# Convolution mixer on one core: the first group's background work is counted at 1.2 times its VectorE time by the planner

## The chip, the core and the metric

The kernel runs on one NeuronCore of a Trainium2 chip. The metric is the device time of one execution in microseconds (us). Three executions of the kernel before gave 2064.7 to 2065.62 us, with a median of 2064.75 us.

## What is computed

The input `x` is (8, 4096, 192) in float32: 8 batches, 4096 tokens, 192 channels. There are three stages.

```python
# 1. causal convolution, 7 taps, one softmaxed filter for each of 8 heads of 24 channels
w = softmax(weight)                                   # (8, 7)
c = einsum('hk,bskhg->bshg', w, windows(x, 7))        # (8, 4096, 192)
# 2. token mixing, weights 4096x256 and 256x4096
u = c + (relu(c.T @ w_tok1) @ w_tok2).T
# 3. channel mixing, weights 192x1536 and 1536x192
out = u + relu(u @ w_ch1) @ w_ch2
```

The four weight matrices arrive as 64-bit floats. The kernel reads them as pairs of 32-bit words and builds float32 values from them on VectorE and ScalarE.

## The kernel before, in words

**Groups and tiles.** The batches are worked on in five groups, `[[0], [1], [2, 3], [4, 5], [6, 7]]`. Within a group the 4096 tokens are cut into 8 tiles of 512. The text below numbers the tiles of the first group (batch 0) 0 to 7 and those of the second group (batch 1) 8 to 15. Each tile goes through the same steps on TensorE (PE):

- `channel1` (L934): 108 matmuls into pairs of PSUM buffers, six pairs. ScalarE (ACT) makes the rounded half `hh` (L973) of each result and VectorE (DVE) the remainder `hl` (L974). One pool of six PSUM buffers, `ps_x`, serves all steps of a tile.
- `mix2` (L861 and L862) for the *next* tile: four blocks of four matmuls each, with the token weights `w_tok2` as the stationary operand. In the first group they come from `t2s`, an SBUF buffer that holds a high part (written by ACT, L185) and a low part (written by DVE, L186). In later groups they come from DRAM as `t`. DVE adds the result to `u` (L876, L877).
- half of `channel2` (L1008, L1009), then `transposed` (L894, with `own` written by ACT at L896 and by DVE at L897) for the next tile, then the other half of `channel2`. DVE adds the results into `osb` (L1012, L1013).

**Background work.** While the first group runs, the kernel must also prepare the second: the convolution of batch 1 on DVE (192 taps at L633; the first tap of each head is on ACT, L631), the first token product of batch 1 on PE (L721), the decoding of the rest of `w_tok2` (12 jobs, each with four steps into `dec_top` at L172, L173, L176, L179 and a last one into the low part of `t2s`, L186), and the copies of the decoded weights to DRAM (`stage`, L1111 on ACT; `t2d`, L1113 on SyncE). In the same manner the second group prepares the third, and so on.

**The planner.** Each engine runs its instructions in the order in which the program was written, so the order is fixed when the kernel is built. A class `Background` decides where a background item goes. It keeps two running sums in nanoseconds, `pe` and `dve`, of the work written so far. After each piece of foreground work, `fg` adds its cost and `fill` puts in items until the DVE sum stands `until` ahead of the PE sum:

```python
if self.dve >= self.pe + until:
    ready = [s for s in ready if s["items"][0].pe]
```

An item of two taps has the cost `2 * (RB * nb * G / 0.96 + 130)`, 660 ns for one batch. Two calls do not ask the budget: `finish(group)` puts in all that is left of a group, and `require(tag)` puts in the items of a stream up to the one with that tag. `require` stands in the first group just ahead of `mix2`, and names the part of `t2s` that this `mix2` reads; each tile of the first group needs two decode jobs more than the tile before it:

```python
if gi == 0 and nxt[0] == 0:
    bg.require(("t2", nxt[1] // 2, nxt[1] % 2))
mix2(*nxt, *loaded)
```

Of the kernel before, what the change touches and what calls it, by code (L numbers as in the profile page):

```python
# [34 lines left out]
class Background:  # L35
# [9 lines left out]
        self.pe = 0.0  # L45
        self.dve = 0.0

    def add(self, items, lead=0.0, group=None):
        total = sum(it.cost for it in items) or 1.0
        self.streams.append(dict(items=items, total=total, done=0.0, free=self.pe, lead=lead, group=group))  # L50

# [63 lines left out]
def conv_mixer_kernel(ctx: ExitStack, tc: tile.TileContext, x, weight, w_tok1, w_tok2, w_ch1, w_ch2, out):  # L115
# [16 lines left out]
    TT = TJ * P  # L132
# [3 lines left out]

    AHEAD = {1: 5, 2: 3}
    LAST = NJ // MJ - 3
    ST = RB * P

    def f32(ap):
        return ap.bitcast(F32)
# [7 lines left out]
    bg = Background()  # L150
# [94 lines left out]
    def t2_job(q2, a0, na, kc=None):  # L245

        c0 = q2 * ST + a0
        cs = slice(2 * c0, 2 * (c0 + na))
# [22 lines left out]
    def decode_items(dec, jobs, loaded=False):  # L271


        n = dec.n / 0.96
        sts = [{} for _ in jobs]
        items = []

        def add(cost, lag, fn, tag=None, gate=None, eager=False):
            items.append(Item(fn, cost + (190 if cost else 0), lag, gate=gate, tag=tag, eager=eager))

        def load(i):
            def fn():
                jb = sts[i]["jb"] = jobs[i][0]()
                sts[i]["raw"] = jb.get("raw") or dec.load(jb["src"], jb["shape"])

            if i < len(jobs):
                add(0, 0, fn, eager=True)

        def begin(i):
            def fn():  # L290
                sts[i]["a"] = dec.a(sts[i], sts[i]["jb"].get("top", lambda: None)())

            if i < len(jobs):
                add(0, 12e3 if i == 0 and not loaded else 0, fn, eager=loaded and i == 0)

        def high(i):
            if not jobs[i][4]:
                return

            def fn():  # L300
                jb = sts[i]["jb"]
                hi, lo = jb["make"]() if "make" in jb else (jb["hi"], jb["lo"])
                sts[i]["b"] = dec.b(sts[i], hi, lo, jb.get("view", lambda v: v))

            add(0, 0, fn, gate=jobs[i][3])

        def low(i):
            def post():
                if "post" in sts[i]["jb"]:
                    sts[i]["jb"]["post"]()  # L310

            if jobs[i][4]:
                add(n, 0, lambda: sts[i]["b"][0](), jobs[i][1])
            add(0, 0, post, jobs[i][1])
            items.extend(jobs[i][2])

        load(0)
        load(1)
        begin(0)
        for i in range(len(jobs)):  # L320
            if i:
                high(i - 1)
            for k, c in enumerate((0.5, 0.5, 1, 1)):
                add(n * c, 500 if k == 0 else 0, lambda i=i, k=k: sts[i]["a"][k]())
                if k == 0 and i:
                    low(i - 1)
                if k == 2:
                    begin(i + 1)
            load(i + 2)
        high(len(jobs) - 1)  # L330
        add(0, 500, lambda: None)
        low(len(jobs) - 1)
        return items
# [264 lines left out]
    def stage1(gi, pools):  # L598
        bs = GROUPS[gi]
        nb = len(bs)  # L600
        convolving, mixing, accs = [], [], []
# [10 lines left out]
        def load(q2, part):  # L612
# [3 lines left out]
            for i, b in enumerate(bs):  # L616

                at = (b * S + q2 * ST - HALO) * D + ds.start
                assert at >= 0
# [40 lines left out]
        def t1_load(n):  # L660
            q2, q = divmod(n, RB // MJ)
            js = slice(q * MJ, (q + 1) * MJ)

            def part(d):
                return d[q2 * ST:(q2 + 1) * ST].rearrange("(p j) t m -> p j t m", j=RB)[:, js]

            top = t1d.rearrange("s (t m) -> s t m", t=1)
            if nb == 1:
                t1 = mp.tile([P, MJ, 1, JT], F32, name="t1", bufs=AHEAD[nb] + 1)
                nc.sync.dma_start(out=t1, in_=part(top))  # L670
            elif gi == 2:
                if n < LAST:
                    t1 = mp.tile([P, MJ, 2, JT], F32R, name="t1", bufs=AHEAD[nb])
                else:

                    if "spare" not in done:
                        done["spare"] = mp.tile([P, 2, ND, TT], F32R, name="other").rearrange("p a c t -> p (a c t)")
                    w = MJ * 2 * JT
                    t1 = done["spare"][:, (n - LAST) * w:(n - LAST + 1) * w].rearrange("p (j t m) -> p j t m", t=2, m=JT)
                nc.sync.dma_start(out=f32(t1[:, :, 1:2]), in_=part(top))  # L680
            else:
                t1 = mp.tile([P, MJ, 2, JT], F32R, name="t1", bufs=AHEAD[nb])
                nc.sync.dma_start(out=f32(t1), in_=part(t1p))
            states[q2]["t1", q] = t1
            mark("t1", n)
# [5 lines left out]
        def t1_lo(q2, q):  # L691
# [3 lines left out]
            nc.gpsimd.dma_start(  # L695
                out=t1p[q2 * ST:(q2 + 1) * ST].rearrange("(p j) t m -> p j t m", j=RB)[:, js], in_=f32(t1)
            )
# [61 lines left out]
        def multiply(*a):  # L759
# [7 lines left out]
            for kc in range(KC):  # L767
# [3 lines left out]
                mixing.append(it)  # L771
            if n + AHEAD[nb] < (LAST if gi == 2 else NJ // MJ):
                mixing.append(Item(lambda: t1_load(n + AHEAD[nb])))
            if gi == 2 and n % 2 and n // 2 < NJ // MJ - LAST:
                mixing.append(Item(lambda: t1_load(LAST + n // 2)))

# [25 lines left out]
            bg.finish(gi)  # L802
            mix1_done(gi, accs)

        bg.add(convolving, group=gi)
        bg.add(second, group=gi)
        return start, finish

# [5 lines left out]
    def t2s_of(q2):  # L814
        if q2 not in t2s:
            t2s[q2] = t2sp[q2 % 2].tile([P, KC, 2, ST], F32R, name="t2s")
        return t2s[q2]
# [236 lines left out]
    td = decode_ctx.enter_context(tc.tile_pool(name="td", bufs=1, side="right", reuse_waits="tile"))  # L1054
# [5 lines left out]
    def first_items():  # L1060

        jobs, stores = [], []
        state = {}

        def decoded(q2):
            state["t2", q2] = max(bg.pe, bg.dve)

        def stored(q2):
            state["stored", q2] = bg.pe

        decoded(0)
        for q2 in range(NS):
            for kc in range(KC):
                for r in range(2):
                    a = (q2, kc, r)
                    stores.append(Item(lambda a=a: store_t2(*a, 0), lag=1000, gate=lambda q2=q2: state.get(("t2", q2))))
                    stores.append(Item(lambda a=a: store_t2(*a, 1), lag=600))
                    stores.append(Item(lambda a=a: store_t2(*a, 2), lag=1200))
            stores.append(Item(lambda q2=q2: stored(q2)))
            for a0 in range(0, ST, TT) if q2 else []:  # L1080
                for kc in range(KC):
                    after = []
                    if a0 + TT == ST and kc == KC - 1:
                        after.append(Item(lambda q2=q2: decoded(q2)))

                    def gate(q2=q2):
                        if q2 > 1 and (mixed[0] <= 2 * (q2 - 2) or ("stored", q2 - 2) not in state):
                            return None
                        return 0.0

                    jobs.append((lambda a=(q2, a0, TT, kc): t2_job(*a), ("t2", q2, a0 // TT), after, gate, True))
        def through():

            decode_ctx.close()
            conv_pool(0)
            starts[2] = stage1(2, lambda k: cps[k])

        stores.append(Item(through))
        bg.add(decode_items(Decoder(td, TT, 2, 2), jobs), lead=0.1, group=1)
        bg.add(stores, group=1)  # L1100

    t2p = []
# [1 line left out]
    def store_t2(q2, kc, r, step):  # L1104

        if step == 0:
            t2p.append(td.tile([P, 2 * TT], F32R, name="stage", bufs=2).rearrange("m (j p) -> m j p", j=RB))
        if step < 2:
            js = slice(step * RB // 2, (step + 1) * RB // 2)
            v = f32(t2s[q2][:, kc, r]).rearrange("m (p j) -> m j p", j=RB)  # L1110
            nc.scalar.copy(out=t2p[-1][:, js], in_=v[:, js])  # L1111
        else:
            nc.sync.dma_start(out=t2d[q2][:, kc, r], in_=f32(t2p[-1]))  # L1113

    def conv_pool(k):
        cps[k] = ctx.enter_context(tc.tile_pool(name=f"cp{k}", bufs=1, reuse_waits="tile"))

    def run_ahead(gi):

        if gi and gi + 2 < len(GROUPS) and gi + 2 not in starts and bg.idle():  # L1120
            starts[gi + 2] = stage1(gi + 2, lambda k: cps[k])
# [101 lines left out]
```

## Time and profile before

| | |
|---|---|
| median of three runs | 2064.75 us (2064.7 to 2065.62) |
| the profiled execution's own time | 2066.69 us |
| its span, first to last instruction | 2064.8 us |
| PE busy | 2052.5 us, 99% of the span |
| DVE busy | 1404.0 us, 68% |
| ACT busy | 760.2 us, 37% |
| mean granted clock of PE | 0.999 |
| the chain that ended last | PE 90%, DVE 6%, DMA 2%, ACT 1% |

The profiled execution's span is 1.9 us shorter than its own time and equal to the median of the three runs to within 0.1 us. "Busy" of PE counts a matmul until its modelled end, and matmuls overlap, so a PE that waits a little can still read as busy. The length of a tile, from the first matmul of its `channel1` to that of the next tile, is the better measure.

### The profile page before, as it was taken

How to read it: one execution, taken by the hardware profiler on the slowest of the kernel's cores; microseconds unless marked ns; L12 is line 12 of the kernel's file. 1: busy time of each engine (PE TensorE's matmuls, PEld its weight loads, DVE VectorE, ACT ScalarE, POOL GpSimd, SP SyncE). 2: the span in 40 equal slices, each digit the busy share in tenths (PEclk: the TensorE clock that was granted, in tenths of full speed). 3: DMA queues.
4: the chain of work that ended last, by engine and by line, in shares of the span. 5: the costliest groups of instructions: out<-in, count | busy, mean ns of one | idle time of the engine just before them, and what ended most of it. 6: DMA issues, size and time to landing. Idle time of an engine off the chain costs nothing.

```text
span 2064.8 us, 41285 instructions
## 1 busy us (share of the span) xinstructions
PE 2052.5 (99%) x17723; PEld 1902.8 (92%) x17723; DVE 1404.0 (68%) x2781; ACT 760.2 (37%) x1305; POOL 101.7 (5%) x167
## 2 busy tenths in 40 slices
PE   9999999999999999999999999999999999999999
PEld 9889999998989989999999999999999999999998
DVE  8899979999559988448965778444445444444444
ACT  4656544434333333224323433233223232233222
POOL 0100000000000000000000000000000000000000
PEclk9999999999999999999999999999999999999999
DMA  9855436554354564232543433322211212222210
GB/s 308 291 154 183 138 120 197 180 164 137 132 160 136 177 170 132 78 103 74 151 124 90 129 122 108 98 60 67 67 45 52 65 50 67 59 67 67 67 32 17
DMA packets 259654, 239.44 MB, mean 116 GB/s; under 512 B 202832, under 2 KB 213584, under 8 KB 257936
## 3 DMA queue, kind: packets, MB, share of 16 engines
q1 hardware_dynamic: 243616, 158.55, 26.6%
q0 software_dynamic: 15856, 78.26, 11.8%
q8 instruction: 140, 2.29, 0.4%
q14 instruction: 42, 0.34, 0.1%
HBM read 146.60 MB, written 71.30 MB: 106 GB/s over the span
## 4 chain that ended last, share of the span: by engine, by line
PE 90%; DVE 6%; DMA 2%; ACT 1%; issue 1%; SPq 0%; POOL 0%; ACTq 0%; POOLq 0%
PE ps_x L934 35%; PE ps_x L1008 16%; PE ps_x L991 16%; PE ps_x L1009 7%; DVE xc L633 2%; PE ps_x L894 2%; PE ps_x L864 2%; PE ps_a L725 2%; PE ps_x L866 2%; PE ps_a L726 2%; PE ps_a L727 2%; PE ps_x L865 2%; DVE hl L974 1%; PE ps_a L426 1%; DMA t2d<-stage 1%; DMA dec_raw<-in_moe_w_tok_dram 1%
## 5 line engine op out<-in xcount | busy, mean ns | idle before, releaser
L973 ACT ACTIVATE hh<-ps_x 128x512 fp32r<-128x512 f32 x756 | 411.1, 597 | 807.2 <-PE ps_x L934 807.1
L974 DVE SCALAR_TENSOR_TENSOR hl<-ps_x,hh 128x512 fp32r<-128x512 f32 x756 | 485.1, 685 | 218.2 <-ACT hh L973 217.7
L934 PE MATMUL ps_x<-own,w_hi 64*128 64x512 f32 x2880 | 607.6, 390 | 1.4 <-DVE hl L974 1.2
L1008 PE MATMUL ps_x<-w,hh 128*128 128x384 f32 x1872 | 542.6, 361 | 0.7 <-DVE hl L974 0.6
L934 PEld LDWEIGHTS ps_x<-own,w_hi 64*128 64x128 f32 x2880 | 429.4, 184 | 55.9 <-issue 6.5
L1009 PE MATMUL ps_x<-w,hl 128*128 128x192 f32 x1872 | 468.8, 250 | 0.0
L934 PE MATMUL ps_x<-other,w_hi 64*128 64x512 f32 x1728 | 450.9, 389 | 0.5 <-DVE osb L1013 0.3
L633 DVE SCALAR_TENSOR_TENSOR xc<-raw,cw,xc 128x384 f32<-128x384 f32 (+1 forms) x768 | 388.7, 561 | 9.2 <-ACT xc L631 9.2
L1009 PEld LDWEIGHTS ps_x<-w,hl 128*128 128x128 f32 x1872 | 357.5, 191 | 0.0
L1008 PEld LDWEIGHTS ps_x<-w,hh 128*128 128x128 f32 x1872 | 351.4, 188 | 1.5 <-DVE hl L974 1.5
L934 PEld LDWEIGHTS ps_x<-other,w_hi 64*128 64x128 f32 x1728 | 314.0, 184 | 33.9 <-DVE hl L974 1.8
L991 PE MATMUL ps_x<-w,hh 64*128 64x384 f32 x2304 | 329.9, 355 | 0.0
L934 PE MATMUL ps_x<-own,w_lo 64*128 64x512 f32 x1440 | 326.5, 387 | 0.0
L991 PE MATMUL ps_x<-w,hl 64*128 64x192 f32 x2304 | 292.2, 247 | 0.1
L934 PE MATMUL ps_x<-other,w_lo 64*128 64x512 f32 x864 | 242.1, 386 | 0.0
L934 PEld LDWEIGHTS ps_x<-own,w_lo 64*128 64x128 f32 x1440 | 218.1, 184 | 24.4
L991 PEld LDWEIGHTS ps_x<-w,hl 64*128 64x128 f32 x2304 | 223.4, 188 | 1.7 <-DVE hl L974 0.8
L991 PEld LDWEIGHTS ps_x<-w,hh 64*128 64x128 f32 x2304 | 219.5, 184 | 0.9
L1012 DVE TENSOR_TENSOR osb<-ps_x,u 128x192 f32<-128x192 f32 x156 | 55.4, 355 | 205.1 <-PE ps_x L1009 204.9
L934 PEld LDWEIGHTS ps_x<-other,w_lo 64*128 64x128 f32 x864 | 159.0, 184 | 16.7
L896 ACT CAST own<-ps_x 128x512 fp32r<-128x512 f32 x120 | 63.4, 595 | 268.7 <-PE ps_x L894 268.5
L999 DVE TENSOR_TENSOR osb<-ps_x,osb 128x192 f32<-128x192 f32 x288 | 103.0, 358 | 17.0 <-DVE osb L999 0.5
(135 smaller groups left out, 1880.4 us busy)
## 6 DMA issues: line engine op xcount, KB each, us to landing
raw<-in_x_dram SPq DMA_DIRECT2D x56, 672.0 KB, 7.4
t<-t2d SPq DMA_DIRECT2D x64, 512.0 KB, 5.0
out_dram<-osb POOLq DMA_DIRECT2D x63, 384.0 KB, 4.3
u<-xcd SPq DMA_DIRECT2D x62, 384.0 KB, 5.6
xcd<-xc POOLq DMA_DIRECT2D x28, 768.0 KB, 7.4
other<-own POOLq DMA_DIRECT2D x24, 768.0 KB, 5.4
t<-t1p SPq DMA_DIRECT2D x32, 512.0 KB, 4.1
t2d<-stage SPq DMA_DIRECT2D x16, 512.0 KB, 4.3
```

The costliest lines, as they stand in the source:

```text
L633: nc.vector.scalar_tensor_tensor(out=dst, in0=src, scalar=cw[:, h, k:k + 1], in1=dst, op0=ALU.mult, op1=ALU.add)
L725: nc.tensor.matmul(out=ps, lhsT=wh, rhs=xh, start=a, stop=False)
L726: nc.tensor.matmul(out=ps, lhsT=wh, rhs=xl, start=False, stop=False)
L896: nc.scalar.copy(out=own[:, 0, c], in_=ps)
L934: nc.tensor.matmul(out=ps, lhsT=w1[w][rows, c, p * P:(p + 1) * P], rhs=t[h][rows, v, c], start=n == 0, stop=n == len(prods) - 1,)
L973: nc.scalar.activation(out=h["hh", f], in_=ps, func=AF.Relu)
L974: nc.vector.scalar_tensor_tensor(out=h["hl", f], in0=ps, scalar=0.0, in1=f32(h["hh", f]), op0=ALU.max, op1=ALU.subtract)
L991: nc.tensor.matmul(out=ps[:, :m], lhsT=h[part, f][ks, ts], rhs=w2[ks, f, :m], start=n == 0 and part == "hh", stop=z and part == "hl",)
L999: nc.vector.tensor_tensor(out=osb[:, j], in0=v, in1=osb[:, j], op=ALU.add)
L1008: nc.tensor.matmul(out=ps[:, :2 * D], lhsT=h["hh", f][:, ts], rhs=w2[:, f, :], start=n == 0, stop=False)
L1009: nc.tensor.matmul(out=ps[:, :D], lhsT=h["hl", f][:, ts], rhs=w2[:, f, :D], start=False, stop=z)
L1012: nc.vector.tensor_tensor(out=rows(osb[:, j]), in0=rows(ps[:, :D]), in1=tokens(u, i)[:, j], op=ALU.add)
```

## The change

`Background.add` gets a factor `pace`, by which the cost of each item of the stream is multiplied. Two streams of the second group get 1.2: the convolution of batch 1 (all but its second raw load, a stream of its own without cost) and the decoding of `w_tok2`. An item of two taps then counts 792 ns instead of 660. What the items compute does not change, and nothing is added to or taken from the program; only the place of the instructions moves.

```diff
-    def add(self, items, lead=0.0, group=None):
+    def add(self, items, lead=0.0, group=None, pace=1.0):
+
+        for it in items:
+            it.cost *= pace
         total = sum(it.cost for it in items) or 1.0
...
+    PACE = 1.2
...
-        bg.add(convolving, group=gi)
+        bg.add(convolving, group=gi, pace=PACE if gi == 1 else 1.0)
         bg.add(second, group=gi)
...
-        bg.add(decode_items(Decoder(td, TT, 2, 2), jobs), lead=0.1, group=1)
+        bg.add(decode_items(Decoder(td, TT, 2, 2), jobs), lead=0.1, group=1, pace=PACE)
```

On every engine the order is the same up to the end of tile 0 and again from the last tile of the second group on. Line numbers behind the edit are four higher in the changed kernel (L974 is L978, L633 is L637). Three places follow.

The first place is DVE at the end of tile 0 and the beginning of `channel1` of tile 1. `xc` rows are taps of the convolution, `osb` is the last sum of tile 0, and the first `hl` row is the first remainder of tile 1. Before:

```order
L633 SCALAR_TENSOR_TENSOR xc_897<-raw_765,cw,xc_897 128x8x24 x2
L957 TENSOR_TENSOR osb<-ps_x,u 128x192
L172 TENSOR_SCALAR dec_top<-dec_top 128x512
L186 TENSOR_TENSOR t2s<-dec_top,t2s 128x512
L173 TENSOR_SCALAR dec_top<-dec_top 128x512
L176 SCALAR_TENSOR_TENSOR dec_top<-dec_raw,dec_top 128x512
L633 SCALAR_TENSOR_TENSOR xc_897<-raw_765,cw,xc_897 128x8x24 x2
L957 TENSOR_TENSOR osb<-ps_x,u 128x192
L633 SCALAR_TENSOR_TENSOR xc_897<-raw_765,cw,xc_897 128x8x24 x2
L179 SCALAR_TENSOR_TENSOR dec_top<-dec_raw,dec_top 128x512
L633 SCALAR_TENSOR_TENSOR xc_897<-raw_765,cw,xc_897 128x8x24 x4
L974 SCALAR_TENSOR_TENSOR hl_934<-ps_x,hh_933 128x512 x2
```

The same stretch in the changed kernel:

```order
L961 TENSOR_TENSOR osb<-ps_x,u 128x192
L637 SCALAR_TENSOR_TENSOR xc_903<-raw_765,cw,xc_903 128x8x24 x2
L176 TENSOR_SCALAR dec_top<-dec_top 128x512
L190 TENSOR_TENSOR t2s<-dec_top,t2s 128x512
L177 TENSOR_SCALAR dec_top<-dec_top 128x512
L180 SCALAR_TENSOR_TENSOR dec_top<-dec_raw,dec_top 128x512
L961 TENSOR_TENSOR osb<-ps_x,u 128x192
L637 SCALAR_TENSOR_TENSOR xc_903<-raw_765,cw,xc_903 128x8x24 x4
L183 SCALAR_TENSOR_TENSOR dec_top<-dec_raw,dec_top 128x512
L978 SCALAR_TENSOR_TENSOR hl_931<-ps_x,hh_930 128x512 x2
```

Ten taps stood ahead of the first `hl`; now there are six.

The second place is DVE in `channel1` of tile 2. The row that writes `t2s` is the last step of the decode job that `mix2` behind this `channel1` reads, in the changed kernel; in the kernel before, that job was done earlier and this row belongs to the next tile's part. Before, from the third `hl` pair to the sixth:

```order
L974 SCALAR_TENSOR_TENSOR hl_1321<-ps_x,hh_1320 128x512 x2
L186 TENSOR_TENSOR t2s<-dec_top,t2s 128x512
L974 SCALAR_TENSOR_TENSOR hl_1323<-ps_x,hh_1322 128x512 x2
L633 SCALAR_TENSOR_TENSOR xc_897<-raw_768,cw,xc_897 128x8x24 x2
L974 SCALAR_TENSOR_TENSOR hl_1323<-ps_x,hh_1322 128x512 x2
L633 SCALAR_TENSOR_TENSOR xc_897<-raw_768,cw,xc_897 128x8x24 x2
L974 SCALAR_TENSOR_TENSOR hl_1325<-ps_x,hh_1324 128x512 x2
L173 TENSOR_SCALAR dec_top<-dec_top 128x512
L176 SCALAR_TENSOR_TENSOR dec_top<-dec_raw,dec_top 128x512
L974 SCALAR_TENSOR_TENSOR hl_1325<-ps_x,hh_1324 128x512 x2
```

The last part of the same `channel1` in the changed kernel:

```order
L978 SCALAR_TENSOR_TENSOR hl_1315<-ps_x,hh_1314 128x512 x2
L183 SCALAR_TENSOR_TENSOR dec_top<-dec_raw,dec_top 128x512
L978 SCALAR_TENSOR_TENSOR hl_1315<-ps_x,hh_1314 128x512 x2
L978 SCALAR_TENSOR_TENSOR hl_1317<-ps_x,hh_1316 128x512 x2
L637 SCALAR_TENSOR_TENSOR xc_903<-raw_768,cw,xc_903 128x8x24 x2
L978 SCALAR_TENSOR_TENSOR hl_1317<-ps_x,hh_1316 128x512 x2
L176 TENSOR_SCALAR dec_top<-dec_top 128x512
L190 TENSOR_TENSOR t2s<-dec_top,t2s 128x512
L637 SCALAR_TENSOR_TENSOR xc_903<-raw_768,cw,xc_903 128x8x24 x2
L880 TENSOR_TENSOR u<-ps_x,u 128x3x64
```

The row into `t2s` moved from among the `hl` rows to behind the last of them. Tile 4 of the changed kernel has the same end: the last two `hl` rows, one row into `dec_top`, one into `t2s`, then taps. In tiles 1, 3, 5 and 6 the row into `t2s` stands ahead of the last `hl` rows.

The third place is PE in tile 2, at the first block of `mix2`, with the semaphores on which each row waits. `h_486` is `h1`, the result of the first token product. Before:

```order
L934 MATMUL ps_x<-own,w_hi 128x512 x6
L861 MATMUL ps_x<-h_486,t2s 128x384 [waits DVE_49]
L862 MATMUL ps_x<-h_486,t2s 128x192
L861 MATMUL ps_x<-h_486,t2s 128x384 [waits Activation_49]
L862 MATMUL ps_x<-h_486,t2s 128x192
```

And in the changed kernel:

```order
L938 MATMUL ps_x<-own,w_hi 128x512 x6
L865 MATMUL ps_x<-h_486,t2s 128x384 [waits DVE_49]
L866 MATMUL ps_x<-h_486,t2s 128x192
L865 MATMUL ps_x<-h_486,t2s 128x384 [waits Activation_49]
L866 MATMUL ps_x<-h_486,t2s 128x192 [waits DVE_49]
```

The fourth matmul now waits for DVE, and all of PE's work behind it stands in the queue after it.

The first product of batch 1 moves as well: of its 128 matmuls, 32 each stood in tiles 2, 3, 4 and 5, and they now stand in tiles 2, 4, 5 and 6.

## Rows read from the trace of the kernel before

**Rows 1.** The page, busy time, share of the span, instructions.

```profile
PE 2052.5 (99%) x17723; PEld 1902.8 (92%) x17723; DVE 1404.0 (68%) x2781; ACT 760.2 (37%) x1305; POOL 101.7 (5%) x167
```

**Rows 2.** Windows, tiles 1-6: length, busy PE, PEld, DVE, ACT, POOL; clock; DMA; GB/s.

```profile
99.62:131.73 32.11, 31.16 (x234) 28.26 (x234) 31.53 (x79) 21.22 (x38) 0.75 (x1) 1.00 0.45 145
131.73:167.03 35.30, 35.30 (x265) 33.47 (x264) 34.62 (x87) 22.78 (x39) 1.31 (x2) 1.00 0.65 196
167.03:202.93 35.90, 35.88 (x265) 32.72 (x265) 35.59 (x90) 19.85 (x37) 1.31 (x2) 1.00 0.50 147
202.93:239.99 37.06, 35.77 (x265) 34.18 (x264) 35.19 (x89) 19.14 (x36) 1.31 (x2) 1.00 0.57 185
239.99:275.14 35.15, 35.15 (x266) 33.75 (x266) 25.11 (x62) 19.25 (x30) 1.85 (x3) 1.00 0.45 144
275.14:305.06 29.92, 29.92 (x234) 28.85 (x234) 26.54 (x55) 11.87 (x25) 1.30 (x3) 1.00 0.20 63
```

**Rows 3.** Chain that ended last, tiles 1, 2 and 5: start us, us, what.

```profile
105.13 1.32 DVE xc L633 x4
106.45 1.20 DVE hl L974 x2
...
165.16 0.33 DVE dec_top L172
...
166.81 0.60 DVE t2s L186
...
240.06 12.50 PE ps_x L934 x108
```

**Rows 4.** Timeline of PE in tile 1: start, us, what [idle before <- releaser].

```profile
107.10 1.33 PE L934 MATMUL ps_x<-own,w_hi 64*128 64x512 f32 x5 [0.84 <-DVE hl L974]
```

**Rows 5.** Timeline of PE, DVE and ACT around `mix2` of tile 4.

```profile
214.43 1.22 ACT L1111 CAST stage<-t2s 128x512 fp32r<-128x512 f32 x1 [1.92 <-DMA t2d<-stage]
...
217.48 0.44 PE L861 MATMUL ps_x<-h,t2s 128*128 128x384 f32 x1 [0.65 <-DVE hl L974]
```

**Rows 6.** Timeline, end of `channel1` and first matmul of `mix2` in tile 3.

```profile
179.90 0.44 PE L861 MATMUL ps_x<-h,t2s 128*128 128x384 f32 x1
...
180.26 0.36 PE L861 MATMUL ps_x<-h,t2s 128*128 128x384 f32 x1
...
180.78 0.42 DVE L172 TENSOR_SCALAR dec_top<-dec_top 128x512 f32<-128x512 f32 x1
181.12 0.68 DVE L186 TENSOR_TENSOR t2s<-dec_top,t2s 128x512 fp32r<-128x512 f32 x1
181.72 1.28 DVE L974 SCALAR_TENSOR_TENSOR hl<-ps_x,hh 128x512 fp32r<-128x512 f32 x2
```

**Rows 7.** Timeline, the same place in tiles 5 and 13.

```profile
252.50 0.44 PE L861 MATMUL ps_x<-h,t2s 128*128 128x384 f32 x1
253.93 1.28 DVE L974 SCALAR_TENSOR_TENSOR hl<-ps_x,hh 128x512 fp32r<-128x512 f32 x2
...
516.03 0.44 PE L861 MATMUL ps_x<-h,t 128*128 128x384 f32 x1
...
516.77 1.29 DVE L974 SCALAR_TENSOR_TENSOR hl<-ps_x,hh 128x512 fp32r<-128x512 f32 x2 [0.53 <-ACT hh L973]
```

**Rows 8.** Timeline, `mix2` of tile 0, whose weights are decoded just ahead of it.

```profile
85.58 0.44 PE L861 MATMUL ps_x<-h,t2s 128*128 128x384 f32 x1 [0.15 <-ACT t2s L185]
86.85 0.35 PE L862 MATMUL ps_x<-h,t2s 128*128 128x192 f32 x1 [0.82 <-DVE t2s L186]
```

**Rows 9.** Windows in the transposes and `channel1` of tile 0; columns as in rows 2.

```profile
58.10:61.50 3.40, 1.72 (x13) 1.20 (x12) 2.85 (x5) 1.31 (x4) 3.40 (x5) 1.00 1.03 409
61.50:64.90 3.40, 3.40 (x17) 2.73 (x19) 2.09 (x4) 2.49 (x4) 3.05 (x5) 0.50 1.03 395
```

**Rows 10.** Windows, tiles 9 and 12 of the second group; columns as in rows 2.

```profile
365.09:399.17 34.08, 34.08 (x258) 32.14 (x258) 32.44 (x65) 14.04 (x27) 1.61 (x3) 1.00 0.50 157
467.33:503.56 36.23, 36.23 (x269) 33.53 (x268) 35.85 (x72) 14.53 (x28) 1.64 (x3) 1.00 0.33 112
```

## Prediction

> **What bounds the kernel now.** The page comes first: PE is busy 99% of the span and DVE 68% [rows 1]. So the time is PE's work plus what PE waits, and an average says nothing of where it waits. The windows by tile do [rows 2]. A tile of the first group without a part of batch 1's product takes 29.92 us (tile 6), and one with 32 of its matmuls 35.15 us (tile 5); in both DVE has room (26.54 and 25.11 us busy). Tiles 1 to 4 are longer than that: 32.11 against 29.92, 35.30 against 35.15, 35.90 against 35.15, 37.06 against 35.15. The excess is 2.19 + 0.15 + 0.75 + 1.91 = 5.00 us. In the same four tiles DVE is busy 31.53, 34.62, 35.59 and 35.19 us, nearly without a gap: it is late, and PE waits for it. The reader should see there that the planner has put too much behind DVE in tiles 1 to 4, and that it runs out of work in tile 5.
>
> The chain and the timelines show the waits themselves. In tile 1 taps end only at 106.45 us, and the first `hl` row follows [rows 3]; PE's fourth pair of `channel1` needs that buffer and starts at 107.10 [rows 4]. In tile 4 an ACT copy into `stage` waits 1.92 us for a DMA, `hh` and `hl` come late behind it, and `mix2` waits at 217.48 [rows 5].
>
> So 5.0 us, 0.24% of the time, is all that a better spread of this work can bring in the first group.
>
> **The change, part by part.** No instruction is added or removed; the sum has only waits that go and waits that come.
>
> *What is relieved.* Back to back a tap takes 0.33 us (four in 1.32), an `hl` row 0.60, a decode step 0.33 to 0.60, say 0.5 on average [rows 3]. By the new order tiles 1 to 4 lose 6, 4, 18 and 6 taps and 1, 3, 4 and 2 decode steps, tile 5 gains 20 and 9. From the measured busy times that makes 31.5 - 2.5 = 29.0, 34.6 - 2.8 = 31.8, 35.6 - 7.9 = 27.7 and 35.2 - 3.0 = 32.2 us of DVE work, in tiles that PE needs 29.92, 35.15, 29.92 and 35.15 us for (tile 3 now has none of batch 1's product, tiles 2 and 4 have 32 each). Tile 5 gets 25.1 + 11.1 = 36.2, but its 25.1 holds what tile 4 left over. Over tiles 1 to 5 together DVE has 162.0 - 14 x 0.33 - 0.5 = 156.9 us to do in 165.3. DVE no longer runs late, so I take the excess of tiles 3 and 4 (0.75 and 1.91) as gone but for 0.15 in all; the `stage` copies of tile 4 now stand ahead of `channel1` of tile 5 rather than inside a `channel1`, and half of `channel2` covers them. Without that cover a DMA that is late would cost the 1.9 us of tile 4 again.
>
> *Tile 1.* Four taps fewer stand ahead of the first `hl`: it starts at 106.45 - 1.32 = 105.1, and the pair is done at 106.3. A `channel1` that does not wait takes 12.50 us for six pairs [rows 3], so PE wants the fourth pair at 99.62 + 6.25 = 105.9: a wait of 0.4 us instead of 1.2. Behind it DVE has 1.20 us of `hl` and 0.66 of taps for each pair against PE's 2.08, so it keeps up. But the last step of the decode job that `mix2` needs now stands behind the tenth `hl` row; it was behind the fourth. Four pairs behind 106.3, at some 1.9 us each, and 0.9 of decode give 114.6 at most, where PE is at `mix2`'s fourth matmul at 113.1: a wait of up to 1.5, I take 1.2. Tile 1 keeps 0.4 + 1.2 = 1.6 of its 2.2 us. Bounds: 0.4 if ACT and DVE are early enough for the decode, 2.2 if nothing is won.
>
> *Tiles 2 and 4.* Here the slower pace meets a due time. `require` finds the job that `mix2` reads unfinished and puts its last steps behind the last `hl` row. The trace of before has the parts of this wait. Call T the first matmul of `mix2`. In tile 3 the same two decode rows stand just ahead of the last two `hl` rows; the four take from 180.78 to 183.00, which is T + 3.1 with T = 179.90 [rows 6]. Put in the other order they end at the same moment. Where nothing stands ahead, in tile 13, the `hl` rows end at 518.06 with T = 516.03, and 0.93 of decode [rows 3] behind them gives T + 3.0; in tile 5 they end at 255.21, which gives T + 3.6 [rows 7]. The fourth matmul could start at T + 0.6 (the third does at T + 0.36) [rows 6]. So PE waits 2.5 us in each of the two tiles; up to 3.1 by tile 5. The only wait for a freshly decoded weight in the trace, in tile 0 with no `hl` row ahead, idled PE 0.82 us [rows 8]; that is the lower bound. It is nearer in name, but tile 3 has the same rows on the same engine, so I take 2.5. Nothing on PE hides it: the matmuls of batch 1 that stand in tile 4's `mix2` are queued behind the waiting one, and so is the rest of the tile. `hl` rows are not delayed by it; what stands behind on DVE (taps, then `u`) is not awaited before the transposes, half a `channel2` later.
>
> *Second group.* Its background work (the convolution of batches 2 and 3) starts about one tile later. By the order, tiles 8 to 12 had 22, 28, 30, 26 and 34 taps; now tiles 8 to 13 have 24, 28, 28, 26, 28 and 30. Tile 12, with the 34 and DVE busy 35.85 of 36.23 us, lost nothing: its 36 matmuls of the token product cost 6.3 over 29.92, at the rate of the 24 in tile 9 (34.08 - 29.92 = 4.16) [rows 2, 10]. So nothing is taken for it; from tile 15 on the order is that of before.
>
> *Sum.* -5.00 + 1.6 (tile 1) + 2.5 + 2.5 (tiles 2 and 4) + 0.15 (the rest) = +1.75 us. The profiled execution took 2066.69 us, of which 2064.8 is span; it would go to 2068.4. The median of the runs is 2064.75, so the forecast there is 2066.5. With all terms at their lower bounds the change is -5.0 + 0.4 + 0.8 + 0.8 = -3.0, with all at their upper +3.5.
>
> **Rivals.**
>
> *A. The due times cost little.* If the decode's steps run while PE is still in `channel1`'s tail, each wait is the 0.82 us of tile 0 [rows 8] or none, and the spread brings what its numbers promise: -5.0 + 1.6 + 1.6 + 0.15 = -1.65, 2063.1; without any wait, 2061.5. For it: DVE then has a gap in each tile. Against it: the two last `hl` rows can't begin before `channel1` ends, and the decode rows are queued behind them.
>
> *B. The waits cost PE its clock.* In tile 0 PE was busy only 1.72 of 3.40 us, and then its granted clock stood at 0.50, the level of 1.2 GHz, for 3.40 us [rows 9]. Half speed for that long costs up to 1.7 us. A wait of 2.5 us leaves PE about as idle as that. The shorter waits in tiles 1 and 4 left the clock at 1.00 [rows 2]. If both new waits are followed by such a stretch the change is 1.75 + 3.4 = +5.2, 2069.9, and slower; with one, 2068.2. It decides where both lose the clock, or one does and the waits are at 3.1.
> The Trainium skill (TensorE: Matmul & The Clock Gate, sections Part 1: The HAM clock gate, and HAM oscillation) says that the clock goes to half after the engine has been idle, and that a kernel whose matmuls wait for data between bursts pays this again after each wait. By that rule the time is the 2069.9 of this rival; the trace agrees at tile 0 and shows no fall at the shorter waits.
>
> *C. The second group pays.* Its work starts later and ends later; if a raw load for batches 2 and 3 lands behind its first tap, ACT's queue holds `hh` and PE waits as in tile 4 (0.65 to 1.9 us) [rows 2, 5], two or three times: +1.75 + 4 = 2070.5. Against it: the taps per tile are fewer than the 34 that cost nothing.
>
> **How the numbers follow.** A difference of about 0.2% (4.1 us) is what a measurement of this kernel can tell from no change. The likeliest case, two new waits that take back a little more than the spread brings, has 0.62 and its own range of 2063.5 to 2068.3; A has 0.14, B 0.15, C 0.09. Faster by more than 0.2% would take the whole 5 us and hardly a wait: a third of A, 0.05. Slower by more: half of B and most of C, 0.15. The rest, 0.80, is within 0.2%. The range runs from A's 2062.5 to 2069.3, short of both falls of the clock.
>
> **What would show it.** In the changed profile the tiles 1, 3 and 5 (which have 0, 0 and 32 matmuls of batch 1) should be near 31.5, 30.0 and 35.2 us, and tiles 2 and 4 near 37.7. PE should show an idle of 2 to 3 us at L866 in tiles 2 and 4, released by the DVE row into `t2s`, and none at `hl` in tile 4. DVE should be busy some 90 to 97% in tiles 1 to 5 instead of 95 to 99% in tiles 1 to 4 and 71% in tile 5. Tiles 8 to 14 should keep their lengths for their number of matmuls. The forecast is wrong if the idle at L866 is short or missing (A), if the granted clock falls behind it (B), or if tiles 7 to 14 grow (C).

## The result, and the profile after

The kernel before took 2064.91 us in the median of 11 runs beside the changed one, the changed kernel 2070.1 us: 1.0022 times as long, with an interval of 1.0014 to 1.0030. It is 5.2 us slower, a small loss, but one clear of no change, since the whole interval lies above 1. The forecast was 2066.5 us and the range ended at 2069.3. The traced execution took 2071.86 us, the longest of the 11, of which 2070.1 is span.

First the page, part 1, as in [rows 1]: the shares don't show the loss.

```profile
PE 2053.4 (99%) x17723; PEld 1900.6 (92%) x17723; DVE 1406.4 (68%) x2781; ACT 761.0 (37%) x1305; POOL 102.2 (5%) x167
```

Then the windows of tiles 1 to 6, with the columns of [rows 2].

```profile
100.91:131.59 30.68, 30.17 (x233) 27.81 (x232) 30.14 (x74) 20.04 (x36) 0.75 (x1) 1.00 0.48 150
131.59:170.86 39.27, 37.24 (x265) 34.07 (x264) 32.87 (x80) 22.55 (x36) 1.31 (x2) 0.96 0.47 152
170.86:200.75 29.89, 29.89 (x235) 27.30 (x234) 27.63 (x67) 13.04 (x27) 0.76 (x1) 1.00 0.35 103
200.75:239.99 39.24, 37.20 (x267) 34.11 (x266) 33.11 (x80) 23.19 (x39) 1.30 (x2) 0.96 0.54 170
239.99:275.11 35.12, 35.12 (x265) 32.48 (x264) 32.26 (x78) 14.65 (x31) 1.30 (x2) 1.00 0.38 118
275.11:310.24 35.13, 35.13 (x265) 34.02 (x264) 23.54 (x56) 18.88 (x30) 2.45 (x4) 1.00 0.51 171
```

Of the 5.3 us by which this span is longer than that of the trace before, 1.3 lie ahead of tile 1, where the order is the same (it begins at 100.91 us instead of 99.62), and 3.9 in tiles 1 to 6 (209.33 us against 205.44). Tiles 3, 5 and 6 take PE's own time (29.92 us without, 35.15 us with 32 matmuls of batch 1's product). Tile 1 has 0.76 us left of its excess. Tiles 2 and 4 are 4.12 and 4.09 us over 35.15, and they alone show a mean clock of 0.96. In each PE is busy 2.1 us longer than in tile 5 for as many matmuls: so part of the excess is not waiting.

The timelines of ACT, DVE and PE at the end of `channel1` in tile 2 show the wait. The first matmul of `mix2` stands at T = 144.08.

```profile
144.18 1.09 ACT L977 ACTIVATE hh<-ps_x 128x512 fp32r<-128x512 f32 x2 [0.95 <-PE ps_x L938]
145.15 0.62 ACT L189 CAST t2s<-dec_top 128x512 fp32r<-128x512 f32 x1
...
144.81 1.29 DVE L978 SCALAR_TENSOR_TENSOR hl<-ps_x,hh 128x512 fp32r<-128x512 f32 x2
146.02 0.42 DVE L176 TENSOR_SCALAR dec_top<-dec_top 128x512 f32<-128x512 f32 x1
146.35 0.68 DVE L190 TENSOR_TENSOR t2s<-dec_top,t2s 128x512 fp32r<-128x512 f32 x1
...
145.83 0.45 PE L865 MATMUL ps_x<-h,t2s 128*128 128x384 f32 x1 [1.22 <-ACT t2s L189]
147.09 0.36 PE L866 MATMUL ps_x<-h,t2s 128*128 128x192 f32 x1 [0.82 <-DVE t2s L190]
```

The decode rows L176 and L190 stand behind the last `hl` pair, as the order said. PE idles twice: 1.22 us until ACT has cast the first part of the weight (ACT's cast is itself queued behind the last `hh` pair) and 0.82 us until DVE has written the second. The fourth matmul starts at T + 3.01, where nothing in the way would have it at T + 0.6. Tile 4 shows the same pair, 1.22 and 0.82 us.

Three windows: the first is that wait, the second the stretch behind it, the third the stretch of the same kind in tile 4:

```profile
144.08:147.09 3.01, 0.98 (x5) 0.48 (x4) 2.92 (x7) 1.59 (x3) 0.00 (x0) 1.00 0.02 5
147.84:151.26 3.42, 3.42 (x15) 3.42 (x14) 2.80 (x10) 1.29 (x4) 0.00 (x0) 0.50 0.02 5
...
216.11:219.52 3.41, 3.28 (x11) 3.28 (x12) 3.38 (x12) 0.35 (x1) 0.00 (x0) 0.50 0.00 0
```

PE was busy 0.98 of 3.01 us, and from 147.84, or 216.11 in tile 4, its granted clock is at 0.50 (1.2 of 2.4 GHz) for 3.41 us. That is the fall of [rows 9], now in the middle of the first group; in the trace of [rows 9] the kernel before has it at tile 0 alone. Below, a fall is such a stretch at half clock.

### The profile page after: what moved, and what is told of

It is laid out like the page before. It is cut to its first block, busy times and chain, and to the rows that moved or that the text cites. A ratio compares the mean times of both kernels' runs of the same rounds, so it can differ in the third digit from the quotient of the medians.

```text
span 2070.1 us, 41279 instructions
## 1 busy us (share of the span) xinstructions
PE 2053.4 (99%) x17723; PEld 1900.6 (92%) x17723; DVE 1406.4 (68%) x2781; ACT 761.0 (37%) x1305; POOL 102.2 (5%) x167
## 4 chain that ended last, share of the span: by engine, by line
PE 94%; DVE 2%; DMA 1%; ACT 1%; SPq 0%; issue 0%; ACTq 0%
PE ps_x L938 37%; PE ps_x L1012 17%; PE ps_x L995 16%; PE ps_x L1013 8%; PE ps_x L898 2%; PE ps_x L868 2%; PE ps_a L729 2%; PE ps_x L870 2%; PE ps_a L730 2%; PE ps_a L731 2%; PE ps_x L869 2%; DMA dec_raw<-in_moe_w_tok_dram 1%; PE ps_x L865 1%; PE ps_a L725 1%; PE ps_a L430 1%; DVE xc L637 1%
## 5 line engine op out<-in xcount | busy, mean ns | idle before, releaser
L978 DVE SCALAR_TENSOR_TENSOR hl<-ps_x,hh 128x512 fp32r<-128x512 f32 x756 | 485.1, 685 | 213.1 <-ACT hh L977 211.1
L637 DVE SCALAR_TENSOR_TENSOR xc<-raw,cw,xc 128x384 f32<-128x384 f32 (+1 forms) x768 | 388.7, 561 | 9.7 <-ACT xc L635 9.6
```

Source lines behind the costliest of these rows:

```text
L637: nc.vector.scalar_tensor_tensor(out=dst, in0=src, scalar=cw[:, h, k:k + 1], in1=dst, op0=ALU.mult, op1=ALU.add)
L978: nc.vector.scalar_tensor_tensor(out=h["hl", f], in0=ps, scalar=0.0, in1=f32(h["hh", f]), op0=ALU.max, op1=ALU.subtract)
```

## Experiments

The theory: the 5 us of excess do go, but two waits for the decoded weight come, and behind each a stretch at half clock, which together cost 8.2 us. The rivals: the low clock costs nothing and the waits alone do it; or the pacing does harm elsewhere (transfers, second group). Each kernel below is the changed one with the edit shown, except the last two, which are the kernel before. Medians are of 11 runs, against the kernel before in the same series: 2065.12 us for TensorE kept at work, the due steps earlier and the two halves, 2065.23 for the change once more, the two with one wait taken away and the pace of 1.3.

**TensorE kept at work through the wait.**

```
@@ mix2, for j in range(TJ)
             ps = ps_x.tile([P, TT], F32, name="ps_x")
+            for _ in range(20 if gi == 0 and q in (3, 5) and j == 0 else 0):
+                nc.tensor.transpose(out=ps[:, 2 * D:], in_=ident, identity=ident)
```

> The changed kernel with 20 transposes of the identity into unused columns of the first buffer of `mix2`, in tiles 2 and 4 only, so that TensorE works while it waits for the decoded weight. Nothing else is moved and nothing read is changed. Theory (each wait of 2.4 us is followed by a stretch at half clock that costs 1.7 us): tiles 2 and 4 fall from 39.3 to some 37.6 us, the granted clock stays at 1.00 in both, and the time is 2066.7 us (2066 to 2067.5). Rival (the low clock is a record without effect, the wait alone costs 4.1 us): 2070, tiles 2 and 4 at 39.2.

Measured: 2067.94 us (2066.2 to 2068.97), 1.0013 of before (1.0004 to 1.0022). The windows of tiles 2 and 4, and the first transposes and the fourth matmul of `mix2` in PE's timeline of tile 2:

```profile
129.80:167.48 37.68, 37.54 (x286) 34.61 (x285) 32.66 (x80) 22.52 (x36) 1.30 (x2) 1.00 0.47 159
197.40:235.04 37.64, 37.53 (x286) 36.21 (x285) 32.90 (x80) 23.00 (x39) 1.30 (x2) 1.00 0.56 177
...
142.29 2.40 PE L857 MATMUL ps_x<-ident 128*128 128x128 f32 x20
...
145.30 0.36 PE L868 MATMUL ps_x<-h,t2s 128*128 128x192 f32 x1
```

The weight is as late as in the change (the fourth matmul of `mix2` starts at 145.30, 3.01 us behind the first transpose at 142.29), but the clock stays at 1.00, and the two tiles are 1.59 and 1.60 us shorter than in the change. So a wait costs 2.5 us over 35.15, as predicted, and the fall behind it 1.6 us. The rival that the clock is harmless is out. This trace has no fall at tile 0 either, where nothing was edited, so by itself it might be a lucky execution. The runs say that it is not: all eleven have a mean granted clock of 0.999 or 1.000, where seven of the change's eleven have 0.998 or less. The median is 0.4 us above the expected band.

**The due steps put in earlier.** The last decode steps are called ahead of the fifth pair of `channel1`, without moving the planner's clock.

```
@@ channel1(t, due=None)
         for p in range(NP):
+            if p == 4 and due:
+                due()
             pss = channel1_mm(t, p)
@@ in the loop over the tiles
-                    h = channel1(abc[i])
+                    due = (lambda: bg.require(("t2", nxt[1] // 2, nxt[1] % 2), True)) if turn and gi == 0 and nxt[0] == 0 else None
+                    h = channel1(abc[i], due)
@@ require(self, tag, soft=False)
-        self.pe = max(self.pe, self.dve)
+        if not soft:
+            self.pe = max(self.pe, self.dve)
```

> The changed kernel with the due decode steps put in ahead of the fifth pair of `channel1` instead of behind the sixth, in the first group only. All else is paced as in the change. Theory (the two waits and what follows them are the whole loss): no idle at the decoded weight in tiles 2 and 4, both at 35.2 to 35.6 us, clock 1.00, and the time is 2062 us (2061.3 to 2063.2), 3 us below the kernel before. Rival (the pacing itself costs, by transfers or by the second group): 2065 or more.

Measured: 2062.63 us (2060.36 to 2063.37), 0.9986 of before (0.9977 to 0.9995). It is the fastest kernel of the study, 2.5 us below the one before and 7.5 below the change. Tiles 1, 2 and 4 in its windows:

```profile
99.75:129.63 29.88, 29.88 (x233) 27.33 (x232) 29.61 (x73) 20.15 (x36) 0.75 (x1) 1.00 0.49 154
129.63:164.74 35.11, 35.11 (x265) 32.46 (x265) 32.28 (x79) 20.45 (x34) 1.30 (x2) 1.00 0.48 157
...
194.78:229.88 35.10, 35.10 (x266) 32.50 (x265) 30.80 (x76) 21.68 (x38) 1.29 (x2) 1.00 0.60 190
```

In tiles 1 to 6 PE waits for nothing that the view of waits lists. So in these tiles the spread itself is free, and the loss of the change comes from where the due steps stand. Behind them the edit also moves some background work to other tiles, and small losses come (tile 7 is 0.36 us over its 30.00, and tile 11 waits 0.2 us for `t`); the gain of 2.5 us is less than the 3.4 to 5.0 us of excess in the traces of the kernel before.

**The change once more**, unedited, beside the next two kernels and the one with the pace of 1.3.

> The changed kernel once more, as it is, beside the next three on one chip. Theory (two waits, each followed by a stretch at half clock in most executions): 2069 to 2071 us, and its own executions lie the higher the lower their mean granted clock: near 2067 without a fall, near 2070.7 with both.

Measured: 2070.49 us (2066.77 to 2071.81), 1.0025 of before (1.0016 to 1.0034). Its trace repeats the first one, with both falls:

```profile
130.62:169.89 39.27, 37.23 (x265) 34.07 (x264) 32.86 (x80) 22.53 (x36) 1.30 (x2) 0.96 0.46 152
...
199.77:239.15 39.38, 37.35 (x265) 34.23 (x264) 33.12 (x80) 23.25 (x39) 1.30 (x2) 0.96 0.56 170
```

In the twelve traces of this study a mean granted clock of 1.000 goes with no fall, 0.999 with one, 0.998 with two and 0.997 with three or four; so the clock that is listed with each run tells roughly how many it had. Of the runs here the three at 0.997 took 2070.5 to 2071.2 us, the four at 0.998 took 2069.0 to 2071.8, and the four at 0.999 took 2066.8 to 2069.4. In the first series, of the result above, the five at 0.997 took 2070.9 us on average and the four at 0.999 and 1.000 took 2067.7. So not every execution has both falls, and 3.2 us between the two ends agrees with two falls of 1.6.

**Only one of the two waits taken away.** The edit is that of the due steps put in earlier, with `and q in (2,)`, or `and q in (4,)`, behind its condition.

> The changed kernel with the due decode steps put ahead of the fifth pair of `channel1` in tile 2 alone; the wait of tile 4 stays. Theory (each wait with its fall costs 4.1 us by itself): tile 2 at 35.1 us, tile 4 at 39.2, clock low once behind tile 0, and 4 us less than the change, 2066 us (2065 to 2067). Rival (the loss is made once, and the other wait then takes it over): tile 4 grows, and 2069 to 2070.

Measured: 2066.2 us (2065.66 to 2067.69), 1.0008 of before (1.0000 to 1.0017), as expected. Tiles 2 and 4:

```profile
130.04:165.15 35.11, 35.11 (x265) 32.45 (x265) 31.93 (x78) 20.44 (x34) 1.30 (x2) 1.00 0.47 155
...
196.42:235.72 39.30, 37.26 (x265) 34.16 (x264) 32.96 (x79) 23.14 (x39) 1.30 (x2) 0.96 0.55 170
```

Each wait is a loss of its own; curing the one in tile 2 does not lengthen the one in tile 4. A smaller wait of 1.1 us came in tile 3 (31.27 us), with the clock at 1.00 behind it.

> The changed kernel with the due decode steps put ahead of the fifth pair of `channel1` in tile 4 alone. By the order, the part of batch 1's product that stood in tile 5 then moves, and in tile 5 the decode's last steps come behind the last `hl` row. Theory: tile 4 is cured, 35.1 us, tile 2 stays at 39.2; whether tile 5 then waits too decides between 2066 us (no wait there) and 2070 (a wait of 2.4 us and a fall, at some 39 us or 34 without the product's matmuls). The order says a wait: 2070.

Measured: 2070.15 us (2067.47 to 2074.69), 1.0023 of before (1.0014 to 1.0032). The wait moved from tile 4 to tile 5, as the order said. Tile 2 was expected at 39.2 us and took 37.68: in this execution the clock did not fall behind its wait. The windows of tiles 2 and 5 are the clearest pair of the study, the same wait in one execution, without the fall and with it:

```profile
129.15:166.83 37.68, 35.64 (x265) 32.48 (x265) 32.67 (x80) 22.65 (x36) 1.30 (x2) 1.00 0.49 159
...
231.87:271.15 39.28, 37.25 (x265) 34.08 (x264) 33.72 (x82) 14.32 (x28) 1.30 (x2) 0.96 0.35 105
```

39.28 - 37.68 = 1.60 us is the fall, all of it in PE's busy time (37.25 against 35.64).

**Half of the change.** Only the convolution paced (the decode's `pace=PACE` dropped), and only the decode paced.

> Only the convolution counted with 1.2 times its time, the decode with its own. By the order the decode row that `mix2` needs then stands behind the last `hl` row in tile 2 alone. Theory: one wait of 2.4 us with one fall of the clock, tile 2 at 39.2 us, tile 4 at 35.2 to 35.6, and 2065.5 to 2066.3 us. Rival 1 (the convolution's pace does the harm): 2069 to 2070. Rival 2 (the decode's pace alone does it): 2061 to 2062.

Measured: 2069.38 us (2066.29 to 2073.04), 1.0020 of before (1.0012 to 1.0029): the number of rival 1, which the theory did not give. The windows of tiles 0, 2 and 12:

```profile
63.62:102.09 38.47, 35.38 (x233) 32.16 (x232) 30.32 (x46) 22.64 (x37) 3.30 (x5) 0.94 0.77 266
...
133.13:172.40 39.27, 36.99 (x265) 34.06 (x264) 34.34 (x83) 22.66 (x37) 1.30 (x2) 0.96 0.48 154
...
469.81:507.84 38.03, 35.75 (x258) 32.88 (x257) 33.36 (x66) 15.86 (x31) 2.55 (x4) 0.96 0.58 188
```

PE's timeline in tile 12, at the start of `mix2`:

```profile
483.80 0.41 PE L865 MATMUL ps_x<-h,t 128*128 128x384 f32 x1 [1.44 <-DMA t<-t2d]
```

The view of waits of SP's queue from 460 to 486 us (in total, times, longest):

```profile
SPq L625 <- DVE xc L637: 13.2, 1, 13.2
```

Tile 2 has its wait and fall, 4.1 us, as expected, and tile 4 has none (tiles 3 and 4 are at PE's time for their matmuls). But tile 12, in the second group, is 3.9 us longer than its 34.1: its weights `t` come late from memory, because their load stands in SP's queue behind a raw load that waited 13.2 us for the taps of its buffer, and the clock falls there too. So in this execution this half does harm in the second group, which the whole change does not (its tile 12 takes 34.07 us). The traced execution is the slowest of the eleven, 2073.04 us, and has one more fall, in tile 0, behind waits of 0.73 and 0.82 us for the decoded weight there. How often the median's runs have these losses is not shown, and the queue as the cause is read from this trace alone.

> Only the decode counted with 1.2 times its time, the convolution with its own. By the order the last decode row stands behind the last `hl` row in tile 2 alone, and only that one row (the step ahead of it stands before the last two `hl`). Theory: a wait of some 1.5 to 2.4 us in tile 2, none in tile 4, tile 3 (36 taps instead of 24) still late by up to 0.8 us: 2064 to 2067 us, the upper end if the clock falls. Rival (the decode's pace does the harm wherever its row stands): 2069 to 2070.

Measured: 2066.66 us (2064.32 to 2069.46), 1.0007 of before (0.9998 to 1.0016). Tile 2 waits 1.9 us for the decoded weight and falls:

```profile
129.24:168.17 38.93, 36.98 (x265) 34.08 (x264) 34.66 (x86) 22.71 (x38) 1.30 (x2) 0.96 0.47 144
```

Tile 3 was not late as I had thought (32.55 us, its matmuls' time); tile 12 waits 1.0 us for `t`, with no fall.

**More of the spread.** The due steps put in earlier, with `PACE = 1.3`.

> Background counted with 1.3 times its time, and the due decode steps ahead of the fifth pair. Theory (with the waits gone nothing is left to win in tiles 1 to 6, which already take TensorE's own time at 1.2): 2062 to 2063.5 us, as at 1.2. Rival (more spread still brings something): 2061 or less. Rival (the later second group now waits for its loads): 2065 or more.

Measured: 2068.78 us (2066.61 to 2071.95), 1.0017 of before (1.0008 to 1.0027): the last rival. Tile 7 in the windows:

```profile
301.04:335.15 34.11, 31.70 (x233) 28.89 (x232) 24.19 (x50) 11.85 (x24) 2.28 (x4) 0.95 0.58 170
```

The timelines of ACT and PE in it:

```profile
315.99 1.12 ACT L636 ACTIVATE xc<-raw,cw 128x384 f32<-128x384 f32 x2 [3.33 <-POOL raw L628]
...
318.44 0.64 PE L1015 MATMUL ps_x<-w,hh 128*128 128x384 f32 x1 [2.41 <-DVE hl L981]
```

An ACT tap waits 3.33 us for its raw tile to be ready (POOL's memset of the halo, which itself waited 1.4 us for the load of that tile), the last `hh` pair is queued behind it, PE idles 2.41 us and its clock falls: 4.1 us over the 30.0 of such a tile. Tiles 6 and 11 wait too, by 0.7 and 1.1 us.

**The kernel before again**, unchanged, in two more traces.

> The kernel before, unchanged, for a second trace. Its first traced execution took 2066.7 us, 1.6 above the median of its timed ones, and showed 5.00 us of excess in tiles 1 to 4. Theory 1 (the excess is the same in each execution, the start of the program differs): tiles 1 to 4 at 32.1, 35.3, 35.9, 37.1 us again, and another time at which `channel1` of tile 1 begins than 99.62 us. Theory 2 (the excess of tile 4, a wait for a DMA, differs): tile 4 at 35.2 to 36 us, and 3 to 4 us of excess.

> The kernel before, unchanged, for a third trace, with the expectations of the second: tile 4 at 37.1 us each time (theory 1) or shorter in some executions (theory 2).

Measured: 2065.38 and 2064.58 us, one run each, near the median where the first trace (2066.69) lay above it. Tiles 1 and 4 of the third trace:

```profile
98.90:130.31 31.41, 30.77 (x233) 28.30 (x232) 31.13 (x78) 20.69 (x37) 0.75 (x1) 1.00 0.45 147
...
201.22:237.69 36.47, 35.64 (x265) 34.09 (x264) 35.18 (x89) 19.17 (x36) 1.30 (x2) 1.00 0.59 188
```

Tiles 1 to 4 take 31.62, 35.55, 35.57 and 36.70 us in the second trace, 31.41, 35.54, 35.37 and 36.47 in the third. Over 29.92 and 35.15 that is 1.70 + 0.40 + 0.42 + 1.55 = 4.07 and 1.49 + 0.39 + 0.22 + 1.32 = 3.42 us, where [rows 2] had 5.00. Neither theory is quite right: the excess differs between executions, in tiles 1, 3 and 4 alike. The third trace has no fall at all, not even at tile 0.

## Why the prediction was wrong

The sign was right (a small loss, +1.75 us), and so were the place of the loss and the wait that makes it; the size was not, and the range ended below the result.

**The step that failed is the weight given to rival B, the fall of the clock.** It was not in the sum, it had a chance of 0.15, and the range was drawn "short of both falls of the clock". What the runs showed in its place is a fall behind most of the new waits, at 1.6 us each, 3.2 us in an execution with both. The price was worked out rightly (up to 1.7 us each); that the rival's 2069.9 us lies so near the 2070.1 measured is partly luck, since two other terms, below, were wrong by 1.3 and 0.8 us in opposite directions.

What was misjudged is which row the new wait is like. The prediction had both: tile 0, where PE was busy 1.72 of 3.40 us and fell [rows 9], and tiles 1 and 4, whose waits of 0.84 and 0.65 us did not fall [rows 2, 4, 5]. A wait in which PE is busy 0.98 of 3.01 us is beyond the first, and should have had the larger chance. Of nine such waits for the decoded weight, of 1.9 us or more, in the traces of the change (twice) and of its variants that left TensorE idle, eight were followed by a fall; the waits of 0.5 to 1.1 us in tiles 1, 3 and 4 were followed by none. In between, the 0.73 and 0.82 us in tile 0 of the convolution-only run were followed by one. No row could have made it certain: four of the twelve traces have no fall at tile 0, where [rows 9] has one.

The Trainium skill (TensorE: Matmul & The Clock Gate, section HAM oscillation) describes a kernel whose matmuls wait for data between bursts and which pays for the cold clock again after each of these waits. In tiles 2 and 4 the trace agrees (clock 0.50 for 3.41 us behind each wait); in tile 2 of the run with tile 4 cured it does not (clock 1.00 behind the same wait).

**The excess of 5.00 us** came from one execution that lay 1.9 us above the median, and the forecast carried that offset over as if it had nothing to do with the excess. The two executions nearer to the median have 4.07 and 3.42, on average 3.7: the prize was over-sized by some 1.3 us, or 0.8 if all three traces are counted (4.2). Why it differs between executions is open.

**Tile 1** was over-sized: 1.6 us predicted, 0.76 measured. `channel1` no longer waits at all (predicted 0.4), and the decode row stands in front of the last `hl` pair and holds `mix2` for 0.51 us (predicted 1.2):

```profile
114.63 0.36 PE L866 MATMUL ps_x<-h,t2s 128*128 128x192 f32 x1 [0.51 <-DVE t2s L190]
```

**Tiles 2 and 4** were right in place and size: 2.5 us each by the run that keeps the clock up, and 2.5 in the one tile 2 without a fall. The releaser was half missed: 1.22 us of each end with ACT's cast, at L865, and only 0.82 with DVE's row at L866.

**The rest**: tiles 3 and 5 at PE's own time and tiles 8 to 14 at the time for their matmuls, as said. The 0.15 us was nothing.

With the measured terms the sum is -3.7 (excess) + 0.8 (tile 1) + 2.5 + 2.5 (waits) + 3.2 (two falls of 1.6) = +5.3 us, and 2064.75 + 5.3 is 2070.05, against 2070.1 measured. That it meets the median this closely is luck: with an excess of 4.2 it would be 0.5 us less, and not every run has both falls.

Of the rivals, A is out (the waits were there in full). C did not happen in this change, but is real: it came with the convolution paced alone, and with a pace of 1.3. The variants' medians agree with such sums only to 1 or 2 us, since the falls and the excess differ from one execution to the next.

## What to carry to other kernels

When work is spread more thinly, look for the due times in it: a step that is forced in at its deadline stands at the worst place, behind everything else in the queue, and here cost more than the spread won. Ask for due work a little earlier (two pairs of matmuls were enough) and the spread keeps its gain.
A wait of TensorE of some 2 us is to be priced with the stretch at half clock that may follow it, 1.6 us here, and a gain read from one trace is to be read from a second one too.

## What the runs showed of the hardware

The granted clock fell for 3.41 us each time, and the fall began 0.75 us after the wait's end in tile 2 (147.84 against 147.09) and 0.13 us before it in tile 4 (216.11 against 216.24): the cost lies in PE's busy time, where a view of waits does not show it. The same wait at the same place of a tile was followed by a fall or not within one execution (tile 5 and tile 2 of the run with tile 4 cured). Twenty transposes whose result nobody reads, in the time of the wait, kept the clock at 1.00 and so saved 1.6 us per tile. What decides whether a given wait is followed by a fall is open.
